# Linear attention followed by a mixture of experts on one core: first-batch loads on one queue, expert loads held behind them, work issued in pieces of four matmuls

## Chip, cores and metric

The kernel runs on one core of one Trainium2 chip. The metric is the device time of one execution in microseconds (us), the median of several runs. The trace of an execution spans some 1.7 to 2.1 us less than the time reported for it, and positions "at 26.24 us" are counted from the start of that span.

## The reference

Eight batches with eight heads of 576 positions go through linear attention with the feature map elu + 1. The result, 4608 rows of 512, goes through all four experts, weighted per row:

```python
q_p, k_p = phi(q), phi(k)                      # phi(x) = elu(x) + 1
kv  = einsum('bhsd,bhse->bhde', k_p, v);  z = sum(k_p, axis=2)
x   = einsum('bhsd,bhde->bhse', q_p, kv) / (einsum('bhsd,bhd->bhs', q_p, z)[..., None] + 1e-6)
# x as (4608, 512)
p   = domain_probs / (domain_probs.sum(-1, keepdims=True) + 1e-9)
out = sum over e of p[:, e:e+1] * (relu(x @ w1[e]) @ w2[e])
```

## The kernel before

The first 512 positions of each batch form one tile of the expert part, so tiles 0 to 7 belong to batches 0 to 7; the 64 left-over positions of all batches form tile 8. While tile j runs its 256 expert matmuls, the attention steps of batch j+1 are issued in between. Batches 0 and 1 have hand-placed steps, because there is nothing, or too little, to hide behind. TensorE (PE), ScalarE (ACT), VectorE (DVE) and SyncE are given their work in the order written. The code below is cut and partly joined into single lines.

```python
ORDER = [("k", 0), ("v", 0), ("q", 0), ("k", 1), ("v", 1), ("q", 1)]   # (tensor, half of the heads)
...
b0.alloc()
b0.load_left("k", eng=nc.scalar)          # the 64 left-over rows
b0.load_left("v", eng=nc.gpsimd)
for n, g in ORDER:
    b0.load(n, g, parts=2 if (n, g) == ORDER[-1] else 1)     # SyncE queue
warm(11)                                  # dummy matmuls
b0.phi("k", 0); b0.vcast(0); b0.left_kv(); b0.kv(0)
for r in range(6):
    load_w(0, r)                          # expert 0, fp32 -> fp16, GpSimd queue
...
for e in range(1, E):
    for r in range(4):
        load_w(e, r)
    if e == 1:
        b0.load_left("q", eng=nc.gpsimd)
b1.load_left("k", "v", "q", eng=nc.gpsimd)
...
T0, TG = 17.0, 0.863                      # a step is issued once T0 + TG * pieces reaches its number
steps = [
    (20.0, emit_probs),
    (40.0, b0.left_q), (40.0, b0.dma_qTl), (45.0, b0.nd_left),
    (50.0, b1.alloc),
    (61.5, b1.left_kv), (62.5, b1.phi, "k", 0), ...     # batch 1's chain, cut
]
...
b1.left_q()
b1.dma_qTl()                              # transposes on the SyncE queue
bts[2].load_left("k", "v", "q")
for n, g in ORDER:
    bts[2].load(n, g)                     # batch 2, behind the transposes on the same queue
for j in range(1, NTILES):
    ...
    run(groups, ([(b1.nd_left,)] if j == 1 else []) + st)   # left-over product first
```

`left_q` computes the feature map of the left-over queries, `dma_qTl` transposes them by DMA, and `nd_left` multiplies them with the key-value matrix on PE. The weights have to come by the GpSimd queue, since the load casts them: the Trainium skill, "DMA: Bandwidth & Descriptors", section "SWDGE vs HWDGE vs iDMA", gives casting loads to that queue alone.

Of the kernel before, what the change touches and what calls it, by code (L numbers as in the profile page):

```python
# [19 lines left out]
def kernel(  # L20
# [16 lines left out]
    P = 128  # L37
# [100 lines left out]
    class Batch:  # L138
# [55 lines left out]
        def vcast(self, g):  # L194
            nc.scalar.copy(  # L195
                self.vp[:, :, g * HG : (g + 1) * HG, 0:D].rearrange("p c h d -> p h c d"),
                self.raw["v", g],
            )
# [47 lines left out]
        def kv(self, g):  # L246
            ps = ppa.tile([P, 2, 2, DE], FP32, tag="aps", bufs=3, name="psum_kv")
            for a in range(2):
                pair = 2 * g + a
                hs = slice(2 * pair, 2 * pair + 2)  # L250
                for c in range(CM):
                    nc.tensor.matmul(  # L252
                        out=ps[:, a],
                        lhsT=self.kp[:, c, hs],
                        rhs=self.vp[:, c, hs],
                        start=(c == 0),
                        stop=False,
                    )
                nc.tensor.matmul(  # L259
                    out=ps[:, a],  # L260
                    lhsT=self.kl[:, pair],
                    rhs=self.vl[:, 2 * a : 2 * a + 2],
                    start=False,
                    stop=True,
                )
            for u in range(2):
                us = slice(u * HP, (u + 1) * HP)
                nc.scalar.copy(
                    out=self.kvz[us, 2 * g : 2 * g + 2, u, :], in_=ps[us, :, u, :]
                )  # L270
# [86 lines left out]
    def layer2_group(j, e, ns, hT):  # L357
        if e == 0:
            accs[j, ns] = pm.tile([P, Dm], FP32, tag="acc", bufs=NACC, name="acc")
        acc = accs[j, ns]  # L360
        py = ppm.tile([P, Dm], FP32, tag="py", bufs=2, name="py")
        for fj in range(FC):
            nc.tensor.matmul(  # L363
                out=py,
                lhsT=hT[fj][:, ns * P : (ns + 1) * P],
                rhs=w2_sb[e][:, fj, :],
                start=(fj == 0),
                stop=(fj == FC - 1),
            )
        pscal = p_sb[:, j, ns, e : e + 1]  # L370
# [24 lines left out]
    def unit(j, e):  # L395
        hT = []
        return [(layer1_group, j, e, fj, hT) for fj in range(FC)] + [
            (layer2_group, j, e, ns, hT) for ns in range(NSUB)
        ]

    def run(groups, steps=()):

        n, m = len(groups), len(steps)
        done = 0
        for i, g in enumerate(groups):
            g[0](*g[1:])
            while done < m and (i + 1) * m >= (done + 1) * n:
                steps[done][0](*steps[done][1:])
                done += 1

    ORDER = [("k", 0), ("v", 0), ("q", 0), ("k", 1), ("v", 1), ("q", 1)]
# [22 lines left out]
    def steps_dma(bt, nxt):  # L434
# [3 lines left out]
        s += [(bt.kv, 0), (bt.kv, 1)]  # L438
# [21 lines left out]
    with tc.manual_schedule(engines={ENG.PE, ENG.Activation, ENG.DVE, ENG.SP}):  # L460
        b0.alloc()
        b0.load_left("k", eng=nc.scalar)
        b0.load_left("v", eng=nc.gpsimd)
        for n, g in ORDER:
            b0.load(n, g, parts=2 if (n, g) == ORDER[-1] else 1)
        warm(11)
        b0.phi("k", 0)
        b0.vcast(0)
        b0.left_kv()
        b0.kv(0)  # L470
        for r in range(6):
            load_w(0, r)
        load_probs(nc.gpsimd)
        warm(1)
        b0.phi("q", 0)
        b0.pe_qT(0)
        b0.pe_qT(1)
        warm(1)
        b0.phi("k", 1)
        b0.vcast(1)  # L480
        b0.nd_pair(0)
        warm(1)
        b0.phi("q", 1, 0, 2)
        b0.kv(1)
        b0.pe_xT(0)
        b0.nd_pair(1)
        b0.phi("q", 1, 1, 2)
        b0.pe_qT(2, nc.scalar)
        b0.pe_xT(1)
        b0.nd_pair(2)  # L490
        b0.pe_qT(3, nc.scalar)
# [6 lines left out]
        for e in range(1, E):  # L498
            for r in range(4):
                load_w(e, r)  # L500
            if e == 1:
                b0.load_left("q", eng=nc.gpsimd)
        b1.load_left("k", "v", "q", eng=nc.gpsimd)
        for n, g in ORDER:
            b1.load(n, g, nc.gpsimd, parts=2 if (n, g) == ORDER[-1] else 1)

        def first_groups(j, hT, phs):
            gs = [(layer1_group, j, 0, fj, hT, phs[fj], range(2, DC)) for fj in range(len(phs))]
            gs += [(layer1_group, j, 0, fj, hT) for fj in range(len(phs), FC)]
            return gs + [(layer2_group, j, 0, ns, hT) for ns in range(NSUB)]  # L510


        T0, TG = 17.0, 0.863
        steps = [
            (20.0, emit_probs),
            (40.0, b0.left_q),
            (40.0, b0.dma_qTl),
            (45.0, b0.nd_left),
            (50.0, b1.alloc),
            (61.5, b1.left_kv),  # L520
            (62.5, b1.phi, "k", 0),
            (64.0, b1.vcast, 0),
            (65.0, b1.kv, 0),
            (66.0, b1.phi, "q", 0),
            (67.0, b1.phi, "k", 1),
            (67.5, b1.pe_qT, 0),
            (67.5, b1.pe_qT, 1),
            (68.5, b1.nd_pair, 0),
            (69.0, b1.vcast, 1),
            (69.0, b1.nd_pair, 1),  # L530
            (70.0, b1.pe_xT, 0),
            (71.0, b1.phi, "q", 1, 0, 2),
            (71.0, b1.kv, 1),
            (71.5, b1.pe_xT, 1),
            (72.0, b1.phi, "q", 1, 1, 2),
            (72.0, b1.pe_qT, 2),
        ]
        done, w = 0, 0
        groups = first_groups(0, hT, phs) + [g for e in range(1, E) for g in unit(0, e)]
        for i, gr in enumerate(groups):  # L540
            gr[0](*gr[1:])
            w += 1 if i % 12 < FC else 2
            while done < len(steps) and T0 + TG * w >= steps[done][0]:
                steps[done][1](*steps[done][2:])
                done += 1
# [4 lines left out]
        phs = [layer1_group(1, 0, fj, hT, None, range(0, 2)) for fj in range(2)]  # L550
        b1.pe_qT(3)
        b1.nd_pair(2)
        phs.append(layer1_group(1, 0, 2, hT, None, range(0, 2)))
        b1.nd_pair(3)
        warm(1)
        b1.pe_xT(2)
        b1.pe_xT(3)
        b1.left_q()
        b1.dma_qTl()
        bts[2].load_left("k", "v", "q")  # L560
        for n, g in ORDER:
            bts[2].load(n, g)
        for j in range(1, NTILES):
            groups = [g for e in range(E) for g in unit(j, e)]
            if j == 1:
                groups[:12] = first_groups(1, hT, phs)
            if j + 1 < B:
                st = steps_dma(bts[j + 1], bts[j + 2] if j + 2 < B else None)
                run(groups, ([(b1.nd_left,)] if j == 1 else []) + st)
            else:  # L570
                run(groups)
# [30 lines left out]
```

## Time and profile before

| | before |
|---|---|
| time, median | 570.94 us (570.79 to 571.06, 3 runs) |
| PE busy | 538.6 us of a span of 568.9 us |
| expert matmuls of tile 0 begin in earnest | 28.37 us |
| expert 3 of tile 0 begins | 76.18 us |
| main stream of tile 1 begins | 102.64 us |
| tile 2 begins | 165.80 us |

The last four are starts of PE groups in the timeline of PE. They cut the front of the kernel into four stretches that can be compared one by one. The windows view over those stretches has, behind the window, its length and the busy time (instructions) of PE, PEld, DVE, ACT and POOL, then the clock granted to PE, the busy share of the DMA engines (a mean that can read above 1), and GB/s:

```profile
0.00:28.37 28.37, 17.37 (x89) 9.59 (x90) 14.79 (x40) 12.51 (x19) 15.61 (x30) 0.64 1.11 223
28.37:76.18 47.81, 43.30 (x190) 19.10 (x189) 9.36 (x15) 14.42 (x25) 14.34 (x24) 0.93 0.96 197
76.18:102.64 26.46, 20.95 (x141) 10.61 (x140) 15.83 (x39) 14.07 (x25) 0.26 (x2) 1.00 0.11 40
102.64:165.80 63.16, 58.57 (x294) 27.23 (x294) 22.58 (x44) 25.67 (x45) 1.07 (x4) 0.97 0.52 141
```

Length less PE busy is PE's idle time: 11.0, 4.5, 5.5 and 4.6 us, 25.6 together. A clock under 1.00 is a second loss, which stands inside the busy time.

### The profile page before, as it was taken

The page shows a single profiled execution, that of the slowest core. Times are in us where ns is not written, and L with a number is a line of the kernel's source. Part 1 is how long each engine was busy: PE and PEld are TensorE (multiplying, and loading weights), DVE is VectorE, ACT ScalarE, POOL GpSimd, SP SyncE. Part 2 cuts the span into 40 slices and gives each one's busy share as a digit, 9 for nine tenths or more (in the row PEclk, how much of TensorE's full clock was granted, in tenths as well). Part 3 has the DMA queues.
Part 4 walks back from the last instruction along what each step waited for, and adds up shares of the span by engine and source line. Part 5 has one row for each costly group of instructions (what it writes and reads, how often), then busy time and mean ns, then how long its engine had stood idle before and what let it go on. Part 6 is the DMA issues. An engine that isn't in the chain of part 4 may idle for free.

```text
span 568.9 us, 7087 instructions
## 1 busy us (share of the span) xinstructions
PE 538.6 (95%) x2703; PEld 253.1 (44%) x2703; DVE 202.5 (36%) x387; ACT 230.8 (41%) x397; POOL 33.9 (6%) x70
## 2 busy tenths in 40 slices
PE   4899797789999999999999999999999999999996
PEld 1543344234544454445444444444445444444442
DVE  3622037253344343433443344334433422222222
ACT  3433244364336433643364336433543333333331
POOL 6442300000000000000000000000000000000000
PEclk7599799899999999999999999999999999999999
DMA  9999802296034503460356035603020300010003
GB/s 226 221 212 215 232 0 75 74 330 145 20 99 154 139 17 100 148 144 11 104 151 143 11 104 152 144 9 103 5 43 10 85 24 0 1 74 1 0 2 74
DMA packets 77730, 54.02 MB, mean 95 GB/s; under 512 B 42960, under 2 KB 70608, under 8 KB 77696
## 3 DMA queue, kind: packets, MB, share of 16 engines
q1 hardware_dynamic: 67888, 41.17, 26.9%
q0 software_dynamic: 9264, 12.27, 11.2%
q8 instruction: 21, 0.34, 0.3%
q10 hardware_dynamic: 544, 0.13, 0.1%
q14 instruction: 13, 0.11, 0.1%
HBM read 45.16 MB, written 9.44 MB: 96 GB/s over the span
## 4 chain that ended last, share of the span: by engine, by line
PE 90%; DMA 3%; DVE 2%; ACT 1%; SPq 1%; issue 1%; POOL 0%; DVEq 0%; POOLq 0%; ACTq 0%
PE ph L344 43%; PE py L363 43%; DMA rl<-in_v_dram 1%; PE psum_kv L252 1%; DMA ql_69<-qlp 1%; PE psum_nd L287 1%; DMA rawb<-in_k_dram 1%; SPq L151 1%; DVE acc L374 1%; DVE x_sb L275 0%; SPq L233 0%; ACT ee L190 0%; PE psum_nl L304 0%; PE psum_kv L259 0%; PE psum_qT L241 0%
## 5 line engine op out<-in xcount | busy, mean ns | idle before, releaser
L353 ACT ACTIVATE ht<-ph 128x512 f16<-128x512 f32 x288 | 168.3, 598 | 298.3 <-PE ph L344 297.7
L363 PEld LDWEIGHTS <-ht 128*128 128x128 f16 x1152 | 111.8, 98 | 134.0 <-ACT ht L353 2.5
L374 DVE SCALAR_TENSOR_TENSOR acc<-py,p_sb,acc 128x512 f32<-128x512 f32 x108 | 81.1, 751 | 165.3 <-PE py L363 165.3
L344 PE MATMUL ph<-xT_all,w_0_80 128*128 128x512 f16 x288 | 68.0, 391 | 0.7 <-ACT xT_all L324 0.7
L344 PE MATMUL ph<-xT_all,w_2_82 128*128 128x512 f16 x288 | 68.4, 390 | 0.0
L344 PE MATMUL ph<-xT_all,w_3_83 128*128 128x512 f16 x288 | 66.6, 379 | 0.0
L363 PE MATMUL py<-w_0_84,ht 128*128 128x512 f16 x288 | 64.0, 379 | 1.7 <-ACT ht L353 1.6
L363 PE MATMUL py<-w_2_86,ht 128*128 128x512 f16 x288 | 64.6, 379 | 0.0
L363 PE MATMUL py<-w_3_87,ht 128*128 128x512 f16 x288 | 64.3, 379 | 0.0
L363 PE MATMUL py<-w_1_85,ht 128*128 128x512 f16 x288 | 63.6, 379 | 0.0
L344 PE MATMUL ph<-xT_all,w_1_81 128*128 128x512 f16 x288 | 63.6, 379 | 0.0
L344 PEld LDWEIGHTS <-w_0_80 128*128 128x128 f16 x288 | 28.4, 101 | 33.8 <-issue 4.2
L344 PEld LDWEIGHTS <-w_1_81 128*128 128x128 f16 x288 | 28.2, 98 | 34.0
L344 PEld LDWEIGHTS <-w_2_82 128*128 128x128 f16 x288 | 28.4, 100 | 32.9 <-issue 3.5
L372 DVE TENSOR_SCALAR acc<-py,p_sb 128x512 f32<-128x512 f32 x36 | 27.0, 749 | 40.9 <-PE py L363 40.9
L344 PEld LDWEIGHTS <-w_3_83 128*128 128x128 f16 x288 | 27.4, 98 | 29.5
L190 ACT ACTIVATE ee<-rawb 128x1024 f16<-128x1024 f32 (+1 forms) x34 | 33.5, 1008 | 5.0 <-DMA rawb<-in_k_dram 4.5
L274 DVE RECIPROCAL recip<-psum_nd 128x6 f32<-128x6 f32 (+2 forms) x52 | 9.6, 184 | 63.5 <-PE psum_nd L287 63.4
L192 DVE TENSOR_TENSOR qp<-ee,qp 128x1024 f16<-128x1024 f16 (+1 forms) x18 | 11.4, 633 | 41.0 <-ACT ee L190 40.5
L275 DVE TENSOR_TENSOR x_sb<-psum_nd,recip 128x384 f16<-128x384 f32 (+2 forms) x52 | 25.3, 486 | 1.8
L195 ACT CAST vp<-rawb 128x1024 f16<-128x1024 f32 x16 | 16.9, 1055 | 2.5 <-DMA rawb<-in_v_dram 2.5
L214 POOL CAST vl<-rl 128x256 f16<-128x256 f32 x8 | 3.5, 435 | 238.1 <-DMA rl<-in_v_dram 238.1
(72 smaller groups left out, 197.1 us busy)
## 6 DMA issues: line engine op xcount, KB each, us to landing
out_dram<-acc SPq DMA_DIRECT2D x32, 256.0 KB, 2.3
rawb<-in_k_dram SPq DMA_DIRECT2D x14, 512.0 KB, 4.1
rawb<-in_v_dram SPq DMA_DIRECT2D x14, 512.0 KB, 4.0
rawb<-in_q_dram SPq DMA_DIRECT2D x13, 512.0 KB, 4.9
w_0_80<-in_moe_w_dram POOLq DMA_DIRECT2D x4, 256.0 KB, 10.9
w_0_84<-in_moe_w_dram POOLq DMA_DIRECT2D x2, 512.0 KB, 12.0
w_1_81<-in_moe_w_dram POOLq DMA_DIRECT2D x2, 512.0 KB, 11.5
w_1_85<-in_moe_w_dram POOLq DMA_DIRECT2D x2, 512.0 KB, 12.7
```

The source lines that it names most:

```text
L151: eng.dma_start(out=self.rl[u * HP : (u + 1) * HP, i], in_=src[b, u * HG : (u + 1) * HG, SM:S].rearrange("h r d -> r h d"),)
L190: nc.scalar.activation(ee[:, 0:n], src, AF.Exp)
L192: nc.vector.tensor_tensor(out=dst, in0=ee[:, 0:n], in1=dst, op=AO.min)
L195: nc.scalar.copy(self.vp[:, :, g * HG : (g + 1) * HG, 0:D].rearrange("p c h d -> p h c d"), self.raw["v", g],)
L252: nc.tensor.matmul(out=ps[:, a], lhsT=self.kp[:, c, hs], rhs=self.vp[:, c, hs], start=(c == 0), stop=False,)
L274: nc.vector.reciprocal(recip[:, 0:n], ps[:, 0:n, :, D:DE])
L275: nc.vector.tensor_tensor(out=dst.rearrange("p n (u d) -> p n u d", u=2), in0=ps[:, 0:n, :, 0:D], in1=recip[:, 0:n].broadcast_to([P, n, 2, ...
L344: nc.tensor.matmul(out=ph, lhsT=w1_sb[e][:, dc, fj * P : (fj + 1) * P], rhs=xT_all[:, dc, j * NT : (j + 1) * NT], start=(dc == 0), stop=(d ...
L353: nc.scalar.activation(ht, ph, AF.Relu)
L363: nc.tensor.matmul(out=py, lhsT=hT[fj][:, ns * P : (ns + 1) * P], rhs=w2_sb[e][:, fj, :], start=(fj == 0), stop=(fj == FC - 1),)
L372: nc.vector.tensor_scalar(acc, py, pscal, None, AO.mult)
L374: nc.vector.scalar_tensor_tensor(out=acc, in0=py, scalar=pscal, in1=acc, op0=AO.mult, op1=AO.add,)
```

## The change

Its intent: let batch 0's loads have the DMA engines to themselves, then the weights; take the left-over product off the path; place batch 1's steps more finely. GpSimd's order is now fixed by hand too.

```diff
-    ORDER = [("k", 0), ("v", 0), ("q", 0), ("k", 1), ("v", 1), ("q", 1)]
+    ORDER = [("q", 0), ("k", 0), ("v", 0), ("q", 1), ("k", 1), ("v", 1)]
...
-        b0.load_left("k", eng=nc.scalar)
-        b0.load_left("v", eng=nc.gpsimd)
         for n, g in ORDER:
             b0.load(n, g, parts=2 if (n, g) == ORDER[-1] else 1)
+            if g == 0 and n != "q":
+                b0.load_left(n)
+        b0.load_left("q")
+        load_probs(nc.sync)
...
+        nc.gpsimd.tensor_copy(gate, b0.raw["q", 1][:, 0, 0, 0:1])     # the hold
+        for r in range(6):
+            load_w(0, r)
...
-    def layer2_group(j, e, ns, hT):            # eight matmuls
+    def layer2_half(j, e, ns, hT, half):       # four matmuls
...
-        T0, TG = 17.0, 0.863
+        T0, TG = 18.5, 0.863
         steps = [
+            (20.0, b0.left_q),
             (20.0, emit_probs),
-            (40.0, b0.left_q),
-            (40.0, b0.dma_qTl),
-            (45.0, b0.nd_left),
+            (22.0, b0.dma_qTl),
+            (40.0, b0.nd_left),
             (50.0, b1.alloc),
... (batch 1's steps in a new order, queries first; value casts of the second half and its kv in halves)
         b1.left_q()
-        b1.dma_qTl()
-        bts[2].load_left("k", "v", "q")
         for n, g in ORDER:
             bts[2].load(n, g)
+        bts[2].load_left("k", "v", "q")
+        b1.dma_qTl()
...
-                run(groups, ([(b1.nd_left,)] if j == 1 else []) + st)
+                run(pieces, st + ([(b1.nd_left,)] if j == 1 else []), 16 if j == 1 else 0)
```

The last argument of `run` keeps the first 16 pieces of tile 1 free of steps.

More of the change, by code (lines that the diff above doesn't have):

```diff
@@ L192, in phi, with vcast @@
             nc.vector.tensor_tensor(out=dst, in0=ee[:, 0:n], in1=dst, op=AO.min)
-        def vcast(self, g):
+        def vcast(self, g, part=0, parts=1):
+            n = HG // parts
+            h0 = g * HG + part * n
             nc.scalar.copy(
-                self.vp[:, :, g * HG : (g + 1) * HG, 0:D].rearrange("p c h d -> p h c d"),
-                self.raw["v", g],
+                self.vp[:, :, h0 : h0 + n, 0:D].rearrange("p c h d -> p h c d"),
+                self.raw["v", g][:, part * n : (part + 1) * n],
             )
@@ L244, in pe_qT, with kv @@
             (eng.copy if eng is nc.scalar else eng.tensor_copy)(out=self.qT[:, :, pair], in_=ps)
-        def kv(self, g):
+        def kv(self, pair0, n=2):
             ps = ppa.tile([P, 2, 2, DE], FP32, tag="aps", bufs=3, name="psum_kv")
-            for a in range(2):
-                pair = 2 * g + a
+            for i in range(n):
+                pair = pair0 + i
                 hs = slice(2 * pair, 2 * pair + 2)
+                a = pair % 2
                 for c in range(CM):
                     nc.tensor.matmul(
-                        out=ps[:, a],
+                        out=ps[:, i],
                         lhsT=self.kp[:, c, hs],
@@ L259, in kv @@
                 nc.tensor.matmul(
-                    out=ps[:, a],
+                    out=ps[:, i],
                     lhsT=self.kl[:, pair],
@@ L268, in kv @@
                 nc.scalar.copy(
-                    out=self.kvz[us, 2 * g : 2 * g + 2, u, :], in_=ps[us, :, u, :]
+                    out=self.kvz[us, pair0 : pair0 + n, u, :], in_=ps[us, 0:n, u, :]
                 )
@@ L355, in layer1_group @@
         return ph
-    def layer2_group(j, e, ns, hT):
-        if e == 0:
-            accs[j, ns] = pm.tile([P, Dm], FP32, tag="acc", bufs=NACC, name="acc")
-        acc = accs[j, ns]
-        py = ppm.tile([P, Dm], FP32, tag="py", bufs=2, name="py")
-        for fj in range(FC):
+    pys = {}
+    def layer2_half(j, e, ns, hT, half):
+        if half == 0:
+            pys[ns] = ppm.tile([P, Dm], FP32, tag="py", bufs=2, name="py")
+        py = pys[ns]
+        for fj in range(half * FC // 2, (half + 1) * FC // 2):
             nc.tensor.matmul(
@@ L369, in layer2_group @@
             )
+        if half == 0:
+            return
+        if e == 0:
+            accs[j, ns] = pm.tile([P, Dm], FP32, tag="acc", bufs=NACC, name="acc")
+        acc = accs[j, ns]
         pscal = p_sb[:, j, ns, e : e + 1]
@@ L393, in layer2_group, with unit, run @@
                     )
-    def unit(j, e):
-        hT = []
-        return [(layer1_group, j, e, fj, hT) for fj in range(FC)] + [
-            (layer2_group, j, e, ns, hT) for ns in range(NSUB)
-        ]
-    def run(groups, steps=()):
-        n, m = len(groups), len(steps)
+    def unit(j, e, hT=None, phs=()):
+        hT = [] if hT is None else hT
+        gs = [(layer1_group, j, e, fj, hT, phs[fj], range(2, DC)) for fj in range(len(phs))]
+        gs += [(layer1_group, j, e, fj, hT) for fj in range(len(phs), FC)]
+        return gs + [(layer2_half, j, e, ns, hT, h) for ns in range(NSUB) for h in range(2)]
+    def run(pieces, steps=(), lead=0):
+        n, m = len(pieces) - lead, len(steps)
         done = 0
-        for i, g in enumerate(groups):
+        for i, g in enumerate(pieces):
             g[0](*g[1:])
-            while done < m and (i + 1) * m >= (done + 1) * n:
+            while done < m and (i + 1 - lead) * m >= (done + 1) * n:
                 steps[done][0](*steps[done][1:])
                 done += 1
-    ORDER = [("k", 0), ("v", 0), ("q", 0), ("k", 1), ("v", 1), ("q", 1)]
+    ORDER = [("q", 0), ("k", 0), ("v", 0), ("q", 1), ("k", 1), ("v", 1)]
     def elementwise(bt, nxt):
@@ L437, in steps_dma @@
         s.append((bt.dma_qTl,))
-        s += [(bt.kv, 0), (bt.kv, 1)]
+        s += [(bt.kv, 0), (bt.kv, 2)]
         def nd(i0, n):
@@ L459 @@
     b0, b1 = bts[0], bts[1]
-    with tc.manual_schedule(engines={ENG.PE, ENG.Activation, ENG.DVE, ENG.SP}):
+    gate = pconst.tile([P, 1], FP32, tag="gate", name="gate")
+    with tc.manual_schedule(
+        engines={ENG.PE, ENG.Activation, ENG.DVE, ENG.SP, ENG.Pool}
+    ):
         b0.alloc()
-        b0.load_left("k", eng=nc.scalar)
-        b0.load_left("v", eng=nc.gpsimd)
         for n, g in ORDER:
             b0.load(n, g, parts=2 if (n, g) == ORDER[-1] else 1)
+            if g == 0 and n != "q":
+                b0.load_left(n)
+        b0.load_left("q")
+        load_probs(nc.sync)
         warm(11)
-        b0.phi("k", 0)
-        b0.vcast(0)
-        b0.left_kv()
-        b0.kv(0)
-        for r in range(6):
-            load_w(0, r)
-        load_probs(nc.gpsimd)
-        warm(1)
         b0.phi("q", 0)
@@ L477 @@
         b0.pe_qT(1)
+        warm(2)
+        b0.phi("k", 0)
+        b0.left_kv()
+        b0.vcast(0)
+        b0.kv(0)
+        nc.gpsimd.tensor_copy(gate, b0.raw["q", 1][:, 0, 0, 0:1])
+        for r in range(6):
+            load_w(0, r)
+        for e in range(1, E):
+            for r in range(4):
+                load_w(e, r)
+        b1.load_left("k", "v", "q", eng=nc.gpsimd)
+        for n, g in ORDER:
+            b1.load(n, g, nc.gpsimd, parts=2 if (n, g) == ORDER[-1] else 1)
         warm(1)
+        b0.nd_pair(0)
+        b0.phi("q", 1)
         b0.phi("k", 1)
-        b0.vcast(1)
-        b0.nd_pair(0)
-        warm(1)
-        b0.phi("q", 1, 0, 2)
-        b0.kv(1)
+        warm(2)
+        b0.pe_qT(2, nc.scalar)
+        b0.nd_pair(1)
+        b0.vcast(1, 0, 2)
+        b0.kv(2, 1)
         b0.pe_xT(0)
-        b0.nd_pair(1)
-        b0.phi("q", 1, 1, 2)
-        b0.pe_qT(2, nc.scalar)
+        b0.pe_qT(3, nc.scalar)
+        b0.vcast(1, 1, 2)
+        b0.kv(3, 1)
+        b0.nd_pair(2)
         b0.pe_xT(1)
-        b0.nd_pair(2)
-        b0.pe_qT(3, nc.scalar)
         b0.nd_pair(3)
@@ L497 @@
         b0.pe_xT(3)
-        for e in range(1, E):
-            for r in range(4):
-                load_w(e, r)
-            if e == 1:
-                b0.load_left("q", eng=nc.gpsimd)
-        b1.load_left("k", "v", "q", eng=nc.gpsimd)
-        for n, g in ORDER:
-            b1.load(n, g, nc.gpsimd, parts=2 if (n, g) == ORDER[-1] else 1)
-        def first_groups(j, hT, phs):
-            gs = [(layer1_group, j, 0, fj, hT, phs[fj], range(2, DC)) for fj in range(len(phs))]
-            gs += [(layer1_group, j, 0, fj, hT) for fj in range(len(phs), FC)]
-            return gs + [(layer2_group, j, 0, ns, hT) for ns in range(NSUB)]
@@ L513 @@
-        T0, TG = 17.0, 0.863
+        T0, TG = 18.5, 0.863
         steps = [
+            (20.0, b0.left_q),
             (20.0, emit_probs),
-            (40.0, b0.left_q),
-            (40.0, b0.dma_qTl),
-            (45.0, b0.nd_left),
+            (22.0, b0.dma_qTl),
+            (40.0, b0.nd_left),
             (50.0, b1.alloc),
-            (61.5, b1.left_kv),
-            (62.5, b1.phi, "k", 0),
-            (64.0, b1.vcast, 0),
-            (65.0, b1.kv, 0),
-            (66.0, b1.phi, "q", 0),
-            (67.0, b1.phi, "k", 1),
-            (67.5, b1.pe_qT, 0),
-            (67.5, b1.pe_qT, 1),
-            (68.5, b1.nd_pair, 0),
-            (69.0, b1.vcast, 1),
-            (69.0, b1.nd_pair, 1),
-            (70.0, b1.pe_xT, 0),
-            (71.0, b1.phi, "q", 1, 0, 2),
-            (71.0, b1.kv, 1),
-            (71.5, b1.pe_xT, 1),
-            (72.0, b1.phi, "q", 1, 1, 2),
-            (72.0, b1.pe_qT, 2),
-        ]
@@ L538 @@
-        done, w = 0, 0
-        groups = first_groups(0, hT, phs) + [g for e in range(1, E) for g in unit(0, e)]
-        for i, gr in enumerate(groups):
-            gr[0](*gr[1:])
-            w += 1 if i % 12 < FC else 2
-            while done < len(steps) and T0 + TG * w >= steps[done][0]:
+            (61.5, b1.phi, "q", 0),
+            (62.5, b1.left_kv),
+            (63.5, b1.phi, "k", 0),
+            (64.0, b1.pe_qT, 0),
+            (65.0, b1.pe_qT, 1),
+            (65.5, b1.vcast, 0),
@@ new lines @@
+            (67.0, b1.kv, 0),
+            (68.0, b1.phi, "q", 1),
+            (68.5, b1.nd_pair, 0),
+            (69.2, b1.phi, "k", 1),
+            (70.0, b1.nd_pair, 1),
+            (70.5, b1.pe_qT, 2, nc.scalar),
+            (70.8, b1.vcast, 1, 0, 2),
+            (71.0, b1.pe_xT, 0),
+            (71.3, b1.pe_qT, 3, nc.scalar),
+            (71.5, b1.vcast, 1, 1, 2),
+            (72.0, b1.pe_xT, 1),
+            (72.5, b1.kv, 2, 1),
+        ]
+        done = 0
+        pieces = unit(0, 0, hT, phs) + [g for e in range(1, E) for g in unit(0, e)]
@@ L544 @@
+        for i, g in enumerate(pieces):
+            g[0](*g[1:])
+            while done < len(steps) and T0 + TG * (i + 1) >= steps[done][0]:
                 steps[done][1](*steps[done][2:])
@@ L549 @@
         hT = []
-        phs = [layer1_group(1, 0, fj, hT, None, range(0, 2)) for fj in range(2)]
-        b1.pe_qT(3)
+        phs = [layer1_group(1, 0, 0, hT, None, range(0, 2))]
+        b1.kv(3, 1)
+        phs.append(layer1_group(1, 0, 1, hT, None, range(0, 2)))
         b1.nd_pair(2)
+        b1.nd_pair(3)
         phs.append(layer1_group(1, 0, 2, hT, None, range(0, 2)))
-        b1.nd_pair(3)
+        b1.pe_xT(2)
         warm(1)
-        b1.pe_xT(2)
         b1.pe_xT(3)
         b1.left_q()
-        b1.dma_qTl()
-        bts[2].load_left("k", "v", "q")
         for n, g in ORDER:
             bts[2].load(n, g)
+        bts[2].load_left("k", "v", "q")
+        b1.dma_qTl()
         for j in range(1, NTILES):
-            groups = [g for e in range(E) for g in unit(j, e)]
-            if j == 1:
-                groups[:12] = first_groups(1, hT, phs)
+            pieces = unit(j, 0, hT, phs) if j == 1 else unit(j, 0)
+            pieces += [g for e in range(1, E) for g in unit(j, e)]
             if j + 1 < B:
                 st = steps_dma(bts[j + 1], bts[j + 2] if j + 2 < B else None)
-                run(groups, ([(b1.nd_left,)] if j == 1 else []) + st)
+                run(pieces, st + ([(b1.nd_left,)] if j == 1 else []), 16 if j == 1 else 0)
             else:
-                run(groups)
+                run(pieces)
 _INS = ['q', 'k', 'v', 'moe_domain_probs', 'moe_w1', 'moe_w2']
```

## The prediction

> **What bounds the kernel now.** I read four views in this order: the slices of the page, the five-microsecond windows, the chain of waits in order of time, and the timeline around each gap. The slices tell where to look.
>
> ```profile
> PE   4899797789999999999999999999999999999996
> ...
> PEclk7599799899999999999999999999999999999999
> ```
>
> One digit is 14.2 us. From the tenth slice on TensorE is full at full clock: nothing to win there except by removing matmuls, and the diff removes none. The tail digit is the last output. Everything the change can win lies before about 117 us. The windows split that stretch:
>
> ```profile
> 50.00:55.00 5.00, 5.00 (x25) 2.27 (x24) 2.56 (x6) 0.00 (x0) 1.00 (x2) 1.00 1.23 207
> 55.00:60.00 5.00, 0.51 (x3) 0.02 (x1) 0.44 (x1) 0.60 (x1) 3.09 (x5) 0.91 1.08 177
> 60.00:65.00 5.00, 4.98 (x15) 2.08 (x16) 0.61 (x2) 1.19 (x2) 2.23 (x7) 0.50 1.04 352
> ```
>
> The columns are length, busy time of PE, PEld, DVE, ACT, POOL (instructions), clock, DMA share, GB/s. PE is idle for 4.5 us and then runs at half clock: 15 matmuls where 25 fit. The chain says why:
>
> ```profile
> 51.90 0.29 DVE qlp L221
> 52.29 0.30 DVE qlp L222
> 52.66 7.32 DMA ql_69<-qlp
> 60.02 0.74 PE psum_nl L304 x4
> 60.77 8.67 PE ph L344 x28
> ```
>
> The left-over queries of batch 0 are computed late (their load sits behind expert 1's weights on the GpSimd queue), their DMA transpose takes 7.3 us beside a saturated weight stream, and TensorE executes in order. The third place is the change from tile 0 to tile 1:
>
> ```profile
> 105.61 0.23 PE L304 MATMUL psum_nl<-kvz_73,ql_75 128*128 128x130 f16 x1 [1.72 <-DMA ql_75<-qlp]
> ...
> 106.97 0.51 PE L304 MATMUL psum_nl<-kvz_73,ql_75 128*128 128x130 f16 x3 [1.14 <-DMA ql_75<-qlp]
> ...
> 114.59 1.06 ACT L190 ACTIVATE ee<-rawb 128x1024 f16<-128x1024 f32 x1 [2.42 <-DMA rawb<-in_k_dram]
> ...
> 116.19 4.11 PE L363 MATMUL py<-w_0_84,ht 128*128 128x512 f16 x17 [1.63 <-ACT ht L353]
> ```
>
> The same left-over product of batch 1 stalls PE twice, and batch 2's first load, issued only at 110.13 because SyncE first sat on the transposes, holds ACT and through it PE. Before 28 us the bound is the serial attention chain of batch 0 at half clock; the expert matmuls proper start at 28.37.
>
> **What the Trainium skill says.** "DMA: Bandwidth & Descriptors", section "Queues, rings and completion order": each DMA engine round-robins between its queue rows packet by packet. The trace agrees; from 12 to 16 us the two queues moved equal packet counts, so the weights take half the turns from batch 0's loads:
>
> ```profile
> q0 software_dynamic: 706, 0.35, 62.7%
> q1 hardware_dynamic: 702, 0.69, 62.4%
> ```
>
> "TensorE: Matmul & The Clock Gate", Part 1: an idle window of about 3.4 us drops the clock to half, and about as long a busy one restores it. The trace agrees: clock 0.50 in 60 to 65 us after 4.5 us idle. Same page, Part 2, "Back-to-back issue gap": the isolated gap at 512 columns is 215.7 ns, but about 131 ns is given for a real stream. The trace has 32 matmuls in 6.91 us, 216 ns; the 131 is not seen. Same page, "Engine queue depths": ACT and DVE are strictly first in, first out; the wait of ht behind ee above shows it.
>
> **The change part by part.**
>
> *Loads and gate.* All batch-0 loads go on the SyncE queue in order q0, k0, left k, v0, left v, q1, k1, v1, left q; weights start after q1. While only such plain loads run (113 to 121 us) the trace moves about 350 GB/s; mixed 257 (12 to 16 us), weights alone about 210 of landed bytes (30 to 55 us). So, starting at 2.0 us as now: q0 (0.52 MB) lands near 4.7, k0 6.2, v0 8.5, left v 9.3, q1 10.8. The gate opens near 11. The remaining 0.6 MB share with weights until about 16, and 0.6 MB of weights land too; the other 7.8 MB at 0.208 MB/us end near 54. Before, the bytes of the windows say weights were in near 55. So holding them costs nothing at the far end. Expert 0's first layer (1 MB) is in by about 20, needed from 22 on; each later expert needs 10 us of stream and gives 13.8 us of matmuls. No weight wait.
>
> *Start chain.* Durations from the timeline: exp 1.05, max/add 0.69, min 0.69, value cast 1.05 (half 0.53), PSUM copies 0.42 (DVE) and 0.59 (ACT), reciprocal plus scaling 0.6 a half pair, a cold group of four transposes or key-value matmuls 0.6. q0 at 4.7 gives both its transposes by 8.2; k0 and left k give keys at 10.5; first kv done 11.3 (now 12.4), kvz 11.95 (now 12.97). Then exps of q1 and k1 end at 14.1, q1 ready on DVE 14.9, k1 16.35, half value cast 16.65, kv of pair 2 17.35, xT0 and qT3 18.6, second half cast 19.75, kv of pair 3 20.4, nd 2, xT1, nd 3 22.2, six partial expert matmuls and two transposes 26.0. With some 15 handovers of 0.05 us: full expert work at 26.8 against 28.37. **Gain 1.5**, the least sure term.
>
> *Middle stall.* The left q is on hand by 16 us, is processed after the second piece, transposed after the fifth (near 30 us), used after piece 25 (near 47). Even 7.3 us, or twice that, is hidden. Gained: 4.5 idle; 28 matmuls in 8.67 instead of 28 x 0.216 = 6.05, 2.6; the four small matmuls 0.74 instead of 0.39. **Gain 7.5.**
>
> *Expert 3 to tile 1.* Now expert 3 starts at 76.18 and tile 1's main stream at 102.64: 26.5. Afterwards the work is 16 pieces x 0.863 = 13.8, six partial matmuls 1.3, batch 1's 68 small matmuls 4.0, a dummy 0.2: 19.3. I placed the steps by their stated times: kv 0 waits 0.6 for the value cast, the DVE line (accumulate 0.75, q1 1.4, normalise 1.2, k1 1.4, accumulate 0.75, normalise 1.2) makes the first xT wait about 2 us for one of three PSUM buffers, nd 0.4, and xT3 about 1.7; with handovers 5.5. So 24.8, **gain 1.7**. Smaller pieces help only by letting steps in between halves.
>
> *First part of tile 1.* The left-over product moves to the tile's end, batch 2's loads go ahead of the transposes, and the first 16 pieces take no step. Gained: 1.7 + 1.1 idle, 20 matmuls in 5.99 instead of 4.32, 1.7, and 1.6 for the late ht, plus 0.2 for cold small ones. **Gain 6.3.**
>
> *Steady tiles.* Matmuls equal: 57.5 us a tile. The last nd step moves from piece 60 to 61 of 64. Now it runs at 162.06, its transpose is issued at 163.48, needed at 166.45. With DVE's accumulate in the way already, I get issue near 163.75 and landing 2.4 later at 166.15: just in time. I allow 0 to 1 us in all.
>
> Sum: 1.5 + 7.5 + 1.7 + 6.3 = 17.0; 570.9 - 17.0 = 553.9, called **554**.
>
> **The rivals.** *A weight wait takes the stall's place.* Against: weights saturate the DMA engines from 16 us in either kernel and end at about the same time. For: the issue to landing of first weights is 9 to 15 us now; if the gate opens at 15 and the pieces still take 10, expert 0 comes at 25 to 30. Time then 557 to 562. *The start gets slower*, since weights no longer use early bandwidth and kv 3 waits for a second half cast: main start at 29 to 30, time 556 to 558. *ACT or DVE becomes the bound* in the twelve microseconds where batch 1's steps now crowd, or batch 1's loads (landing about 60 to 68, wanted from 69) come late: 3 to 5 us lost, 557 to 559. *The transition is better than placed*: my 5.5 us of waits could be 2, time 550. *The transfer of the left queries was hidden anyway*: excluded, PE waited for it by name.
>
> **Range and chances.** The middle and tile-1 terms, 13.8 together, are waits read by name with nothing in the new order that waits there; the other two, 3.2, carry an error of about 4 between them. Hence 549 to 560, eight in ten. The 2% line is 570.94 / 1.02 = 559.7; one rival alone hardly reaches it, two together do. Faster by over 2%: 0.87; within: 0.12; slower: 0.01.
>
> **What would show it.** In the changed profile: only the hardware queue moves bytes until about 11 us, at 300 or more GB/s; full expert matmuls begin at 25.5 to 28; no PE gap and no half clock between 30 and 66; no weight named as a releaser of PE; expert 3 starts at 66 to 68; gaps of about 5 us with DVE and PSUM-buffer releasers up to 92; none from 93 to 117. Wrong it would be if PE waits for w_0_80, if the transposes still take their place on PE near 47, or if each tile boundary shows a new wait for xT.

## The result

The changed kernel took 551.18 us (550.58 to 551.34, 4 runs); the kernel before took 571.0 us in the same rounds. The ratio is 0.9646, with a 95% interval of 0.9630 to 0.9663: 3.5% less. A ratio here compares the fast runs of both kernels in the same rounds, so it is not quite the ratio of the two medians. All ratios below are against the kernel before of the same rounds.

The slices of the page after, to be read against those shown before: PE is short of full only in the first two slices, the sixth and the last; the hole at the fifth slice is gone, and so are the low clocks at the fifth and the eighth.

```profile
PE   6799989999999999999999999999999999999996
...
PEclk8599999999999999999999999999999999999999
```

The windows after, cut at the same events, in the same columns:

```profile
0.00:26.24 26.24, 17.97 (x92) 9.46 (x92) 13.82 (x35) 12.70 (x21) 12.70 (x26) 0.69 1.12 236
26.24:66.65 40.41, 40.41 (x189) 18.41 (x189) 10.39 (x18) 14.29 (x25) 12.69 (x21) 0.99 1.10 234
66.65:90.02 23.37, 20.68 (x141) 10.67 (x140) 14.67 (x35) 15.19 (x29) 0.26 (x2) 1.00 0.20 68
...
90.02:146.26 56.24, 56.24 (x294) 26.88 (x293) 22.67 (x44) 25.95 (x45) 0.93 (x4) 1.00 0.54 151
```

PE's idle time is now 8.3, 0, 2.7 and 0 us. The spans differ by 568.9 - 549.3 = 19.6 us; 14.6 of that is idle time (25.6 - 11.0), the rest the half clock that followed the gaps.

All in us:

| stretch | before | after | gain | predicted |
|---|---|---|---|---|
| start to full expert work | 28.37 | 26.24 | 2.1 | 1.5 |
| to expert 3 | 47.81 | 40.41 | 7.4 | 7.5 |
| to tile 1's main stream | 26.46 | 23.37 | 3.1 | 1.7 |
| to tile 2 | 63.16 | 56.24 | 6.9 | 6.3 |
| tile 2 to the end | 403.1 | 403.0 | 0.1 | 0 to -1 |

The gate and what came after it, in the timeline of GpSimd: the copy waits for the query half, and weights are issued from 9.99 us on.

```profile
8.42 0.73 POOL L216 CAST vl<-rl 128x256 f16<-128x256 f32 x1 [6.04 <-DMA rl<-in_v_dram]
9.86 0.19 POOL L491 COPY gate<-rawb 128x1 f32<-128x1 f32 x1 [0.71 <-DMA rawb<-in_q_dram]
9.99 3.12 POOL L99 DMA_DIRECT2D w_0_80<-in_moe_w_dram  x4
```

In brackets stands how long the engine was idle before the row, and for what. GpSimd waited 6.04 us for the left-over values and only 0.71 us for the gate: a detail to be tested.

The place of the middle stall, after. The first line is from the view of the tile `ql_69`, the transposed left-over queries (durations in ns, then first and last start); its last line gives the time from issue to landing:

```profile
L307 PE MATMUL psum_nl<-kvz_67,ql_69 x4: 218/219/220, 46.6 to 46.7; 128*128 128x130 f16 x4
...
DMA to landing us min/median/max: 5.5/5.8/6.1
```

The transposes, issued at 28.7 us, still take 5.5 to 6.1 us beside the weight stream, but the product comes at 46.6 us, long after, at full clock and without a wait.

### The profile page after: what moved, and what is told of

It reads as the page before. It is cut to its first block, busy times and chain, and to the rows that moved or that the text cites. A ratio compares the mean times of both kernels' runs of the same rounds, so it can differ in the third digit from the quotient of the medians.

```text
span 549.3 us, 7084 instructions
## 1 busy us (share of the span) xinstructions
PE 533.6 (97%) x2705; PEld 252.0 (46%) x2705; DVE 201.9 (37%) x381; ACT 234.3 (43%) x403; POOL 28.7 (5%) x64
## 4 chain that ended last, share of the span: by engine, by line
PE 94%; DVE 3%; ACT 1%; DMA 1%; issue 0%; DVEq 0%
PE ph L347 45%; PE py L367 45%; PE psum_kv L255 1%; PE psum_nd L290 1%; DVE x_sb L278 1%; DMA rawb<-in_q_dram 1%; PE psum_kv L262 0%; DVE acc L383 0%; DVE qp L192 0%; PE psum_qT L243 0%; PE psum_xT L326 0%; PE psum_nl L307 0%; ACT xT_all L327 0%; DVE qp L191 0%; ACT kvz_67 L271 0%
## 5 line engine op out<-in xcount | busy, mean ns | idle before, releaser
L347 PE MATMUL ph<-xT_all,w_0_80 128*128 128x512 f16 x288 | 66.6, 386 | 0.7 <-ACT xT_all L327 0.7
L367 PE MATMUL py<-w_3_87,ht 128*128 128x512 f16 x288 | 66.1, 379 | 0.0
L347 PE MATMUL ph<-xT_all,w_3_83 128*128 128x512 f16 x288 | 66.1, 379 | 0.0
L367 PE MATMUL py<-w_2_86,ht 128*128 128x512 f16 x288 | 65.7, 379 | 0.0
L347 PE MATMUL ph<-xT_all,w_2_82 128*128 128x512 f16 x288 | 64.4, 379 | 0.0
L367 PE MATMUL py<-w_1_85,ht 128*128 128x512 f16 x288 | 63.8, 379 | 0.0
L347 PE MATMUL ph<-xT_all,w_1_81 128*128 128x512 f16 x288 | 63.7, 379 | 0.0
L367 PE MATMUL py<-w_0_84,ht 128*128 128x512 f16 x288 | 63.6, 379 | 0.0
L190 ACT ACTIVATE ee<-rawb 128x1024 f16<-128x1024 f32 x32 | 33.3, 1051 | 2.8 <-DMA rawb<-in_q_dram 2.4
L192 DVE TENSOR_TENSOR qp<-ee,qp 128x1024 f16<-128x1024 f16 x16 | 11.1, 692 | 23.2 <-ACT ee L190 22.4
L192 DVE TENSOR_TENSOR kp<-ee,kp 128x1024 f16<-128x1024 f16 x16 | 11.1, 692 | 21.6 <-ACT ee L190 21.2
L197 ACT CAST vp<-rawb 128x1024 f16<-128x1024 f32 (+1 forms) x18 | 17.3, 960 | 0.5 <-DMA rawb<-in_v_dram 0.5
```

Source lines behind the costliest of these rows:

```text
L190: nc.scalar.activation(ee[:, 0:n], src, AF.Exp)
L192: nc.vector.tensor_tensor(out=dst, in0=ee[:, 0:n], in1=dst, op=AO.min)
L197: nc.scalar.copy(self.vp[:, :, h0 : h0 + n, 0:D].rearrange("p c h d -> p h c d"), self.raw["v", g][:, part * n : (part + 1) * n],)
L347: nc.tensor.matmul(out=ph, lhsT=w1_sb[e][:, dc, fj * P : (fj + 1) * P], rhs=xT_all[:, dc, j * NT : (j + 1) * NT], start=(dc == 0), stop=(d ...
L367: nc.tensor.matmul(out=py, lhsT=hT[fj][:, ns * P : (ns + 1) * P], rhs=w2_sb[e][:, fj, :], start=(fj == 0), stop=(fj == FC - 1),)
```

## The experiments

Twelve kernels ran; all were correct. Except for the last (12), each is an edit of the changed kernel, so it has to be held against 551.2 us, ratio 0.9646.

How small a difference can be read? The changed kernel did not run again in the rounds of the experiments; only the kernel before did, with medians of 570.6 to 571.0 us. Also, seven of these kernels have the same start (the changed one and 3, 4, 5, 6, 7, 9), and in their profiles full expert work begins anywhere from 25.43 to 26.30 us. In the early ones the clock is back at 1.00 from 25 us on; in the changed kernel, at 26.24, it is 0.55 from 25 to 27 us. So differences under about 1 us from 551.2 us, or between the starts of two single profiles, are not resolved here.

**1. No gate.**

```diff
-        nc.gpsimd.tensor_copy(gate, b0.raw["q", 1][:, 0, 0, 0:1])
```

> The changed kernel without the gate copy, nothing else. In its profile GpSimd had already waited until 8.4 us for the left values, because the cast of them stands before the weight loads in its program; the gate itself waited 0.71 us more. Theory A: the gate as such is worth almost nothing, because the cast holds the weights anyway: first weight issue near 9.2 instead of 9.99 us, time 551 (550.5 to 552). Rival B: the gate is what makes the start faster: weights would take turns from q1, k1 and v1, and the time goes up by 1 to 2 us.

Measured: 550.35 us, ratio 0.9649 (0.9611 to 0.9688): theory A, 0.15 us under its range. The gate as such does nothing that can be measured. The timeline of GpSimd without it:

```profile
8.82 0.60 POOL L216 CAST vl<-rl 128x256 f16<-128x256 f32 x1 [6.43 <-DMA rl<-in_v_dram]
9.36 3.13 POOL L99 DMA_DIRECT2D w<-in_moe_w_dram  x4
```

Weights start at 9.36 instead of 9.99 us: the cast of the left-over values, which stands before them in GpSimd's program, holds them.

**2. Weights first.** No gate, and expert 0's loads moved ahead of everything GpSimd waits for.

```diff
-        nc.gpsimd.tensor_copy(gate, b0.raw["q", 1][:, 0, 0, 0:1])
-        for r in range(6):
-            load_w(0, r)
...
+        for r in range(6):
+            load_w(0, r)
         warm(11)
         b0.phi("q", 0)
```

> No gate, and the six loads of expert 0 issued ahead of everything that GpSimd waits for, so from about 2.3 us. Theory A (holding the weights matters, by whatever holds them): in mixed traffic the plain queue of the kernel before got 0.69 MB in 4 us, half its pace alone, so k0 lands near 8, v0 near 12, q1 near 16, and the full expert work starts 3 to 4 us later than 26.24: 554 to 556. Rival B (the start chain is bound by engines and half clock, not by loads): below 1 us, 551 to 552.

Measured: 559.45 us, ratio 0.9811 (0.9770 to 0.9851): 8.3 us lost, twice what theory A expected. Full expert work begins at 33.54 instead of 26.24 us. The timeline of ACT names what it waited for, and the queue view of 8 to 14 us (packets, MB, share of the engines' time) says why:

```profile
11.49 1.05 ACT L197 CAST vp<-rawb 128x1024 f16<-128x1024 f32 x1 [2.36 <-DMA rawb<-in_v_dram]
...
20.80 1.06 ACT L190 ACTIVATE ee<-rawb 128x1024 f16<-128x1024 f32 x1 [2.97 <-DMA rawb<-in_k_dram]
```

```profile
q0 software_dynamic: 1195, 0.59, 71.7%
q1 hardware_dynamic: 1217, 0.80, 57.0%
```

The two queues take turns packet by packet (1195 and 1217 packets), as in the section of the Trainium skill that the prediction cites, and batch 0 gets 0.80 MB in 6 us, 133 GB/s. In the changed kernel the same queue alone moved 1.38 MB from 5 to 9 us, 344 GB/s. The first value half is cast at 11.49 instead of 7.69 us, the second key half arrives at 20.80. Of the 8.3 us, 7.3 are there at the first stretch; expert 3 starts 8.4 us later (75.06 against 66.65), because the routing weights, last on the SyncE queue, now also came late and DVE waited 5.8 us for them, PE 1.1 us for DVE.

**3. Left-over queries loaded early, processed late.** The load stays where the change put it; only the steps return to the distance they had.

```diff
-            (20.0, b0.left_q),
             (20.0, emit_probs),
-            (22.0, b0.dma_qTl),
-            (40.0, b0.nd_left),
+            (42.0, b0.left_q),
+            (42.0, b0.dma_qTl),
+            (46.5, b0.nd_left),
```

> The left queries of batch 0 still loaded early on the SyncE queue, but processed after piece 28 and their product placed after piece 33, the distance that the kernel before had. Theory A (the place of the steps makes the stall, five pieces being shorter than the transpose beside the weight stream): the stall of 4.5 us and the half clock come back, plus 7 us, about 558, ql_69 named as releaser. Rival B (the late load made it): no stall, 551. Either way the load itself is on hand long before.

Measured: 558.25 us, ratio 0.9783 (0.9735 to 0.9831), 7.1 us lost. The chain of waits has the old picture back:

```profile
50.71 7.22 DMA ql<-qlp
...
57.98 0.71 PE psum_nl L307 x4
58.69 8.79 PE ph L347 x28
```

So nearly all of the middle term (7.1 of 7.4 us) is a matter of distance between the transpose and its use. The kernel before shows the same. Its left-over queries were issued at 26.19 us and landed 10.1 to 10.4 us later, by 37.3; the step that uses them came at 48.33 and did not wait for them:

```profile
26.19 1.26 POOL L151 DMA_DIRECT2D rl<-in_q_dram  x2 [1.95 <-DMA w_0_84<-in_moe_w_dram]
...
48.33 0.41 ACT L219 ACTIVATE elq<-rl 128x256 f16<-128x256 f32 x1
```

The early load makes a step as early as the changed kernel's possible. Whether a step soon after 37 us would have been early enough without it was not tested.

**4. Tile 1 undone.**

```diff
+        b1.dma_qTl()
+        bts[2].load_left("k", "v", "q")
         for n, g in ORDER:
             bts[2].load(n, g)
-        bts[2].load_left("k", "v", "q")
-        b1.dma_qTl()
...
-                run(pieces, st + ([(b1.nd_left,)] if j == 1 else []), 16 if j == 1 else 0)
+                run(pieces, ([(b1.nd_left,)] if j == 1 else []) + st, 0)
```

> In tile 1 alone the old order: the transposes of batch 1's left queries ahead of batch 2's loads, their product as the first step, no free pieces at the front. Theory A: the 6.9 us between the two kernels from 102.64 to 165.80 and from 90.02 to 146.26 come back, 557 to 558.5, with the same three waits. Rival B (part of the 6.9 came from the earlier stages, which leave the engines in better order): 553 to 555.

Measured: 557.42 us, ratio 0.9774 (0.9734 to 0.9815), 6.2 us lost; the waits view of 88 to 120 us names the same two releasers as before, for three waits (total, times, longest, in us):

```profile
PE psum_nl L307 <- DMA ql<-qlp: 1.9, 2, 1.1
...
PE py L367 <- ACT ht L356: 1.7, 1, 1.7
```

It is 0.7 less than the 6.9 of the table. In its profile the stretch takes 62.11 us (89.77 to 151.88), 1.05 less than before, and the trace shows the larger part of why: the first wait for `ql` is 0.85 us here against 1.72 before, since the first step now comes after four pieces, ten matmuls, where it came after six matmuls.

**5. No free pieces.**

```diff
-                run(pieces, st + ([(b1.nd_left,)] if j == 1 else []), 16 if j == 1 else 0)
+                run(pieces, st + ([(b1.nd_left,)] if j == 1 else []), 0)
```

> The changed kernel without the sixteen free pieces at the front of tile 1; the loads stay ahead of the transposes and the left-over product stays last. Theory A (the place of the product and the order of the loads do it, the free pieces are a margin): batch 2's q0 was issued at 86.68 and is in before the step near 93.5, 551 to 551.7. Rival B (the free pieces keep ACT clear of late loads): 552 to 554, with ht waiting behind ee.

Measured: 550.48 us, ratio 0.9645 (0.9632 to 0.9657). After the main stream of tile 1 has begun, PE waits for nothing in that tile. The sixteen free pieces are a margin and gain nothing here.

**6. Left-over product first, loads early.**

```diff
-                run(pieces, st + ([(b1.nd_left,)] if j == 1 else []), 16 if j == 1 else 0)
+                run(pieces, ([(b1.nd_left,)] if j == 1 else []) + st, 0)
```

> As the changed kernel, batch 2's loads ahead of the transposes, but batch 1's left-over product as the first step of tile 1 and no free pieces. Theory A (the product must stand far from its transpose; loads ahead of the transposes make the distance worse): the transposes are issued behind the last load, near 97, land after 100, and PE waits from about 93.5: 7 to 10 us lost with the half clock, 558 to 561, more than with the whole of tile 1 undone (557.4). Rival B (only the late loads cost time in tile 1): 551 to 553.

Measured: 563.46 us, ratio 0.9869 (0.9851 to 0.9887): 12.3 us lost, more than expected and twice as much as with all of tile 1 undone. The timeline of PE:

```profile
99.61 0.29 PE L307 MATMUL psum_nl<-kvz,ql 128*128 128x130 f16 x1 [8.19 <-DMA ql<-qlp]
101.25 0.51 PE L307 MATMUL psum_nl<-kvz,ql 128*128 128x130 f16 x3 [1.35 <-DMA ql<-qlp]
```

With batch 2's loads ahead, SyncE issues the transposes only at 96.55 us. Here, moving the loads ahead of the transposes without also moving the product was worse than changing nothing in tile 1. (The free pieces, also gone in this run, are shown by experiment 5 to matter nothing.)

**7. Whole groups in tile 0.**

```diff
             g[0](*g[1:])
+            if g[0] is layer2_half and g[-1] == 0:
+                continue
             while done < len(steps) and T0 + TG * (i + 1) >= steps[done][0]:
```

> The changed kernel, with the steps of tile 0 let in only after whole groups of eight second-layer matmuls instead of after halves. Theory A (halves help only by letting steps in between them): some steps of batch 1 come up to 0.86 us later, 0.5 to 2 us lost between expert 3 and tile 1, 551.5 to 553. Rival B (pieces of four give all of the 3.1 us that this stretch gained): 553.5 to 554.5. Rival C: no difference, 551.

Measured: 551.23 us, ratio 0.9657 (0.9639 to 0.9674); the stretch from expert 3 to tile 1 takes 23.76 us (66.31 to 90.07) against 23.37. The time is rival C's, no difference; the pieces of four, named in the title, give some 0.4 us in this stretch by one profile of each kernel. By elimination most of its 3.1 us come from the new order and places of batch 1's steps; no run undid these alone.

**8. More dummies.** A try at a faster kernel.

```diff
         b0.pe_qT(1)
-        warm(2)
+        warm(8)
...
-        warm(1)
+        warm(2)
         b0.nd_pair(0)
         b0.phi("q", 1)
         b0.phi("k", 1)
-        warm(2)
+        warm(10)
...
         b0.nd_pair(1)
+        warm(4)
...
         b0.pe_qT(3, nc.scalar)
+        warm(5)
```

> A try at a faster kernel: dummy matmuls fill the gaps of the start chain (8, 2, 10, 4 and 5 in place of 2, 1, 2, 0 and 0), so that the clock does not fall to half at 9.9 us. Theory A (the start chain is partly bound by the half clock): groups of four transposes 0.4 instead of 0.6, six partial matmuls 0.216 instead of 0.427: 2 to 4 us less, 547 to 549. Rival B: the dummies stand in the chain's way or the clock falls all the same: 551 to 553.

Measured: 549.06 us, ratio 0.9615 (0.9597 to 0.9632), 2.1 us gained. The windows of the changed kernel and of this one, in the columns as above:

```profile
10.00:15.00 5.00, 2.96 (x19) 1.57 (x17) 3.22 (x8) 2.53 (x4) 5.00 (x8) 0.50 1.28 253
```

```profile
10.00:15.00 5.00, 4.05 (x31) 2.19 (x32) 3.64 (x8) 2.68 (x5) 5.00 (x7) 1.00 1.30 261
```

The clock stays at 1.00 and full expert work begins at 23.32, 2.9 us sooner than in the profile of the changed kernel and 2.1 sooner than in the earliest of the seven with its start. In the profiled execution 1.3 us of that were given back at one tile boundary: a transpose of x landed 4.2 us after its issue, where the usual time is 2.4, and PE waited for it. (The ratio's interval meets that of the changed kernel; the times, 548.25 to 549.43 against 550.58 to 551.34, do not.) Experiment 11 takes that up.

**9. Batch 1 earlier.** The new T0 moves every step of tile 0 six pieces forward, batch 0's left-over steps too.

```diff
-        T0, TG = 18.5, 0.863
+        T0, TG = 23.5, 0.863
...
             (72.5, b1.kv, 2, 1),
+            (73.3, b1.kv, 3, 1), (74.2, b1.nd_pair, 2), (75.0, b1.nd_pair, 3),
+            (76.0, b1.pe_xT, 2), (77.0, b1.pe_xT, 3),
... (the same five calls, the dummy and the partial matmuls in front of tile 1 removed: phs = [])
```

> A try at a faster kernel: all steps of batch 1 six pieces sooner (its loads are in by 67 us, the steps begin at 67.5) and the rest of its chain inside tile 0 too, so that no partial matmuls are needed. Theory A (the 2.7 us that PE idles between 66.65 and 90.02 come from the chain being crowded at the end): 548.5 to 549.5. Rival B (ACT, which has eight evictions of 0.6 us in the same stretch, becomes the bound): 551 to 553.

Measured: 547.85 us, ratio 0.9595 (0.9575 to 0.9615), 3.3 us gained by the medians, 2.9 by the ratios; PE had idled 2.7 us there. One PE wait of 0.9 us (for a DVE scaling) is left in the stretch. ACT did not become the bound.

**10. Both.** The edits of 8 and 9 together.

> The two tries together: more dummies in the start chain (2.1 us alone) and batch 1's chain earlier and wholly inside tile 0 (3.3 alone). Theory A (they act in different stretches and add): 545.5 to 546.3. Rival B (tile 0 now starts 2.9 us sooner while batch 1's loads do not, so ACT waits for them): 547 to 548.

Measured: 545.60 us, ratio 0.9563 (0.9548 to 0.9578). The two gains, 2.1 and 3.3, add to 5.4; 5.6 were measured, the same within the scatter. One late transpose of x was seen again (1.1 us).

**11. Both, and steps spread over two pieces fewer in later tiles.**

```diff
-        n, m = len(pieces) - lead, len(steps)
+        n, m = len(pieces) - lead - 2, len(steps)
```

> As e10_both, and in every later tile the steps are spread over two pieces fewer, so that the last transpose is issued 1 to 2 us sooner before the tile that needs it. In e8_more_dummies one boundary showed a transpose that landed 4.2 instead of 2.4 us after its issue and held PE for 1.3 us. Theory A: that was one odd boundary of one run; no change against e10_both beyond 0.5 us. Theory B: such late landings occur in every run; 0.5 to 1.5 us less than e10_both.

Measured: 544.71 us, ratio 0.9545 (0.9532 to 0.9558), 0.9 us less than experiment 10 of the same rounds, and no wait for x in the profile. The intervals of the two ratios touch, though the slowest run of this one (545.33) is under the fastest of the other (545.38). Only one execution of each was profiled: that late landings occur in every run is likely but not shown. This is the fastest kernel: 4.5% under the kernel before and about 1% under the changed one.

**12. The kernel before, with the weights held.** GpSimd's order was fixed by hand, as in the change; the instruction lists of the other engines are unchanged. This matters: GpSimd's order in the kernel before was not fixed, and its timeline has three loads of expert 0 ahead of the cast that stands before them in the text:

```profile
3.61 2.27 POOL L99 DMA_DIRECT2D w_0_80<-in_moe_w_dram  x3
10.87 0.66 POOL L214 CAST vl<-rl 128x256 f16<-128x256 f32 x1 [5.00 <-DMA rl<-in_v_dram]
```

So the fixed order holds these loads behind the cast, and the gate holds them longer; the run does not separate the two.

```diff
-    with tc.manual_schedule(engines={ENG.PE, ENG.Activation, ENG.DVE, ENG.SP}):
+    with tc.manual_schedule(engines={ENG.PE, ENG.Activation, ENG.DVE, ENG.SP, ENG.Pool}):
...
+        nc.gpsimd.tensor_copy(gate, b0.raw["q", 1][:, 0, 0, 0:1])
         for r in range(6):
             load_w(0, r)
```

> The kernel before with one thing added: a one-column copy on GpSimd that waits for the second query half of batch 0, ahead of the weight loads. All other engines keep their order word for word. Theory A (holding the weights is by itself what makes the start faster, the order of the six loads matters little): left values land near 8 instead of 10.8, the first kv ends 2 us sooner, full expert work near 26 instead of 28.37, time 568.5 to 569.5; the middle stall and the one in tile 1 stay. Rival B (the gain of the start came from taking the queries first): 570.5 to 571.5.

Measured: 568.05 us (564.89 to 569.99), ratio 0.9950 (0.9927 to 0.9974). In the profile full expert work begins at 26.62 instead of 28.37 us. The hold (fixed order and gate together) thus gives 1.75 us of the first stretch by these two profiles. The time is 2.5 us less by the medians (1.5 to 4.2 us by the interval), a little more than theory A expected. What the queries in front and the single queue add to that can't be told from nothing, with starts that vary by 0.9 us.

The profiled execution, the slowest of the six, kept little of this. It was 2.2 us ahead when tile 1's main stream began (100.48 against 102.64 us) and lost 1.8 of it in tile 1. There PE waited 2.08 us for `ht`, and the clock was 0.57 from 114 to 118 us; the kernel before waited 1.63 us at that place and stayed at 1.00. The runs of this kernel scatter over 5 us (564.89 to 569.99), as those of the kernel before did in the rounds of experiments 1 to 4 (566.90 to 572.43).

## Why the prediction was right

The time, 551.18 us, lies in the predicted range, 2.8 us under the 554 that was called. The terms add to 17.0 us against 19.6 in the traces. Three of the four came within 0.6 us, by the mechanism that was read; in the fourth the kind of wait was right and the sizes were not. By its steps:

- **Loads and gate.** Right: plain loads ran alone at 310 to 384 GB/s from 3 to 12 us, the weights started at 9.99, and no weight was named by PE. Experiments 2 and 12 show that the hold matters. What the prediction did not see is that the gate itself is nearly idle (experiment 1). It put the plain loads at 350 GB/s, and they were a little faster: the second query half was in by 9.86 us, not 10.8.
- **Start chain**, 1.5 predicted, 2.1 measured, inside its stated error. Starts that vary by 0.9 us without any edit don't settle the term better than that.
- **Middle stall**, 7.5 predicted, 7.4 measured. One sentence of it was wrong: "computed late (their load sits behind expert 1's weights on the GpSimd queue)". Experiment 3 had the load early and the stall all the same, and in the kernel before the queries had been there for 11 us when the step came; the place of the steps was the cause. The term held because the change moved both.
- **Expert 3 to tile 1**, 1.7 predicted, 3.1 measured: the mis-sized term of the sum. The working put 5.5 us of waits there, and PE idled 2.7. Its 19.3 us of work were too few, PE was busy for 20.68, so two errors partly cancelled. The largest item, "about 2 us for one of three PSUM buffers", took 0.67 us and had another releaser; PE's timeline after has:

```profile
81.48 0.38 PE L326 MATMUL psum_xT<-identh,x_sb 128*128 128x128 f16 x4 [0.67 <-ACT qT L246]
```

  The transpose waited for the copy of the third query transpose, not for the scaling of the second pair, so the buffers were not taken in the strict turn that the working assumed. "Smaller pieces help only by letting steps in between halves" was right in tone, and experiment 7 puts the help at 0.4 us or less.
- **First part of tile 1**, 6.3 predicted, 6.9 measured. The prediction named three causes at once. The experiments weigh them: the free pieces gain nothing (5); loads ahead of the transposes do harm as long as the product comes first (6). Not tested were late loads with the product last. One reading was incomplete: batch 2's first load was late not only "because SyncE first sat on the transposes". In the timeline of SyncE these took 2.44 us from 103.30 on, and six loads of left-over rows 4.1 us more, to 110.03. The change moved both behind the large loads, and no run separates the two.
- **Steady tiles**, a loss of 0 to 1 allowed, a gain of 0.1 measured. The margin of 0.3 us that was worked out held in the changed kernel. That it is thin showed in experiments 8 and 10, each with one boundary where PE waited for the transpose.
- **Rivals.** None of the losses came. The last but one, that the transition is better than placed, did; its 1.4 us are half of what carried the time to the lower side of the range.

## What to carry to other kernels

Work off the end of the critical path must also be placed at a distance from its use that its slowest transfer, under the load of that moment, needs; look for the distance before you move loads. Keep bulk loads that are needed late behind small ones that are needed first, and check what really holds them: here a cast in the issuing engine's program did it, and the gate did not. Where a serial chain leaves PE with gaps, dummies that fill them can pay through the clock (experiment 8), and steps that wait at the end of a tile should be tried a few pieces sooner.

## What the Trainium skill lacked or had wrong

- "DMA: Bandwidth & Descriptors" has no figure for loads that cast. Weights cast from fp32 to fp16, alone on the engines from 30 to 50 us of the kernel before, landed at 212 GB/s (4.24 MB of fp16) with the engines fully busy. Each landed byte is two bytes read, so this is about 424 GB/s of reading, by estimate; plain loads moved 344 to 401.
- The same page, "Where 436 GB/s comes from": its note lets about 358 GB/s bind between HBM and SBUF, though the table just before it has more for one core with large loads. The table is borne out here, the note is not. Batch 1's loads ran at 397 to 401 GB/s in single microseconds at 60 to 62 and 64 to 66 us of the changed kernel.
- The same page, on transposes by DMA, gives rates but no latency beside other traffic: a transpose of the left-over queries landed 5.4 to 7.3 us after its issue within the weight stream (all profiles), and the transposes of x in later tiles took 2.4 us by the median.
- "TensorE: Matmul & The Clock Gate", "Back-to-back issue gap": about 131 ns for 512 columns in a real stream is not seen; 32 matmuls without a step between them take 6.91 us, 216 ns each, in the later tiles of all fourteen profiles (single groups up to 7.04).
